# A kernel of attention, a gated FFN and a SoLU FFN: a new order of all its steps

## The chip, the cores and the metric

The kernel runs on one core of a Trainium2 chip. The metric is the device time of one execution in microseconds (us). Each measurement has several runs, and the median is taken.

## The reference

```python
scores = scale * np.matmul(rotate(q), rotate(k).transpose(0, 1, 3, 2))   # 2 batches, 8 heads, 576 tokens, 64 wide
attn = np.exp(scores - np.max(scores, axis=-1, keepdims=True))
attn = attn / (np.sum(attn, axis=-1, keepdims=True) + 1e-09)
x = np.matmul(attn, v)                            # -> 1152 tokens x 512
x = (x @ w_a) * (x @ w_b) @ w_out                 # 512 -> 1536 -> 512
h = x @ w_in                                      # 512 -> 1024
e = np.exp(h - np.max(h, axis=-1, keepdims=True))
solu = h * e / (np.sum(e, axis=-1, keepdims=True) + 1e-09)
ln = (solu - mu) / np.sqrt(var + 1e-06) * g_ln    # mean and variance over the 1024
out = ln @ w_out2                                 # 1024 -> 512
```

`rotate` is the rotary embedding by tables of cosines and sines. All data is float32.

## The kernel before, in words

**Precision.** Nearly every operand of a matrix product is kept as two parts, a high part (a rounded copy, made by ScalarE) and a low part (the rest, made by a subtraction on VectorE or GpSimd). A product takes three matmuls: high by high, high by low, low by high.

**Attention** works on eight units, each a pair of heads of one batch. A unit has nine tiles of 64 or 128 score rows, 72 tiles in all. Tile n passes through `qk.n` (scores, L444), `mx.n` (row maximum on VectorE, L453), `ex.n` (exponential on ScalarE, L461), `tp.n` (transposes, L474), `ph.n` and `pl.n` (high and low part, L488 and L492). Then come the products with V: `pv00_0.u` to `pv11_3.u` are, for four blocks of unit u, the first five matmuls, the last four (both L523), ScalarE's copy of one half of the result (L530) and VectorE's sum with the other half (L537). Beside this run the loads (`lk.u`, `lq.u`, `lv.u`, issued on SP's queue), the rotary steps (`rk`, `rq`) and the normalised rows of x (`xd`, L599 to L603).

**The gated FFN** computes part of its products by a Strassen-like scheme with seven products instead of eight, which needs sums of x: `s1`, `s3` and `sb` (L746, by way of L833 to L843) write the tiles `sums_f`. The columns of the first weight tiles are made plainly: `AB.f.t` (L715) fills a PSUM slot with both products, `ab.f.t` (L819) copies one to SBUF, `g.f.t` (L822) multiplies it by the other and so empties the slot. Weights come in by large loads (`ld`), are unpacked in integer steps (`p1` to `p4`, L173 to L181) and split (`hi`, `lo`, L192 and L195).

**The SoLU FFN** uses the same kind of scheme: `Q1` to `Q7` (L1130) are its products of six matmuls a piece, `q1` a copy of PSUM on ScalarE (L1137), `S..`, `Sh`, `Sl` the sums and their parts, `u` and `ul` those of the weights. Then `hx`, `he`, `hm`, `hs`, `hn` (L1158 to L1184) normalise a block of rows, `L` transposes it (L1192), `lh` and `ll` split it, and `O` (L1228) is the output product, whose weight's parts are made by `hj` (L792) and `lj` (L746).

**The order.** All of it is in one list of 1816 words, `SCHEDULE` (L35 to L141). A word is a step with its indices; a last `.1` puts the step on GpSimd where both engines can do it. The kernel walks through the list and calls the step of each word, and every engine's queue keeps the order in which the words issue to it:

```python
ctx.enter_context(tc.manual_schedule())                       # L205
...
def tt_(out_, a, b, op, eng=0):                               # L745
    (nc.vector, nc.gpsimd)[eng].tensor_tensor(out_, a, b, op=op)
...
def s1_a(k, eng=0):
    tt_(f_slot(0, k), _raw(x_part(k, 0)), _raw(x_part(2 + k, 0)), plus, eng)
def s3_a(k, eng=0):
    tt_(f_slot(2, k), _raw(x_part(k, 1)), _raw(x_part(k, 0)), sub, eng)
def s_b(j, k, eng=0):
    tt_(f_slot(j, k, 1), f_slot(j, k, 0), f_slot(j, k, 1), plus, eng)
...
for word in SCHEDULE.split():                                 # L1278
    name, *args = word.split(".")
    ...
    fn(*args)
```

So nothing but the list sets which instruction stands behind which on an engine; between engines, semaphores hold an instruction until its inputs are written and its buffer is free.

Of the kernel before, what the change touches and what calls it, by code (L numbers as in the profile page):

```python
# [20 lines left out]
B, H, S, D = 2, 8, 576, 64  # L21
# [14 lines left out]
wm1.0 rka0.0 ll.0 rka1.0 rka2.0 rkr0.0 rkr1.0 rkr2.0 rqx0.0 rqx1.0 rqx2.0 wm2.0 kha.0 kla.0 kA_0.0 rqa0.0 rqa1.0  # L36
kA_1.0 rqa2.0 qdx.0 qAx0.0 rkb0.0 qda.0 R_0.0 R_1.0 qA_0.0 qAh0.0 rkb1.0 rkb2.0 khb.0 rqb0.0 wm3.0 rqb1.0 qAh1.0
rqb2.0 cs.0 qAl0.0 qk.0 wm4.0 qAl1.0 qdb.0 R_2.0 mx.0 rq0.1 klb.0 lk.2 qk.1 mx.1 rq1.1 rq2.1.1 kB_0.0 rk0.1 ex.0
ex.1 qk.2 kB_1.0 mx.2 qB_0.0 qB_1.0 qd.1 qk.3 mx.3 rk1.1 tp.0 qB_2.0 tp.1 ex.2 ph.0 pl.0 ex.3 rk2.1.1 qk.4 mx.4
ph.1 t4A_0.0 rk0.2.1 lq.2 tp.2 t4A_1.0 t4A_2.0 kh.1 kl.1.1 lv.0 qA_0.1 ph.2 qA_1.1 qk.5 lv.1 pl.1 tp.3 ex.4 ph.3  # L40
mx.5 ex.5 vh.0 qk.6 pl.2 lk.3 vl.0.1 t4R_0.0 qA_2.1 rk1.2.1 t4R_1.0 rk2.2.1 kB_0.1 tp.4 mx.6 qk.7 pl.3 t4R_2.0
kB_1.1 tp.5 kA_0.1 mx.7 ph.4 pl.4 R_0.1 ex.6 qk.8 kA_1.1 mx.8 ph.5 pv00_0.0 pv00_1.0 tp.6 R_1.1 ex.7 R_2.1 ex.8
ph.6 qk.9 qk.10 lv.2 sa.0 pl.5 pv01_0.0 pv01_1.0 kh.2 rq0.2 mx.9 ex.9 qB_0.1 pv00_2.0 rq1.2.1 rq2.2.1 pv01_2.0
# [1277 lines left out]
```

## Time and profile before

| what | us |
|---|---|
| median of 3 runs | 482.96 |
| lowest and highest | 482.83, 483.72 |
| the profiled execution | 483.67 |
| its span | 481.9 |

The span runs from the first to the last instruction that the profile records; the execution's own time holds 1.77 us more. In the profile each instruction has a start and a duration. A time in square brackets behind a row is how long the engine stood idle before it, with the work whose end released it. PE is TensorE, DVE is VectorE, ACT is ScalarE, POOL is GpSimd, SP is the engine that issues most loads.

### The profile page before, as it was taken

The page shows a single profiled execution, that of the slowest core. Times are in us where ns is not written, and L with a number is a line of the kernel's source. Part 1 is how long each engine was busy: PE and PEld are TensorE (multiplying, and loading weights), DVE is VectorE, ACT ScalarE, POOL GpSimd, SP SyncE. Part 2 cuts the span into 40 slices and gives each one's busy share as a digit, 9 for nine tenths or more (in the row PEclk, how much of TensorE's full clock was granted, in tenths as well). Part 3 has the DMA queues.
Part 4 walks back from the last instruction along what each step waited for, and adds up shares of the span by engine and source line. Part 5 has one row for each costly group of instructions (what it writes and reads, how often), then busy time and mean ns, then how long its engine had stood idle before and what let it go on. Part 6 is the DMA issues. An engine that isn't in the chain of part 4 may idle for free.

```text
span 481.9 us, 8469 instructions
## 1 busy us (share of the span) xinstructions
PE 469.0 (97%) x3109; PEld 442.6 (92%) x3109; DVE 416.4 (86%) x634; ACT 344.6 (72%) x651; POOL 191.0 (40%) x157
## 2 busy tenths in 40 slices
PE   8899999999999989999999999999999999999997
PEld 7799999989989989999999999999999778888886
DVE  6999999999999699998998699787699999878671
ACT  4899999989898356787778887778886554434322
POOL 1799979789263200012152520222203586411100
PEclk9999999999999999999999999999999999999999
DMA  5532463241120415213235643454430220100002
GB/s 119 129 90 82 124 162 80 55 124 50 27 91 23 128 48 176 88 47 129 88 122 184 219 156 113 170 175 156 133 150 1 88 87 2 44 23 22 23 22 65
DMA packets 47351, 45.94 MB, mean 95 GB/s; under 512 B 24336, under 2 KB 41295, under 8 KB 46799
## 3 DMA queue, kind: packets, MB, share of 16 engines
q1 hardware_dynamic: 46366, 44.53, 30.2%
q10 hardware_dynamic: 944, 0.89, 0.6%
q8 instruction: 24, 0.39, 0.4%
q14 instruction: 17, 0.13, 0.1%
HBM read 39.01 MB, written 4.49 MB: 90 GB/s over the span
## 4 chain that ended last, share of the span: by engine, by line
PE 78%; DVE 10%; ACT 5%; POOL 3%; issue 2%; DMA 1%; SPq 0%; DVEq 0%; POOLq 0%; ACTq 0%
PE x L1012 16%; PE out L1228 10%; PE pb L942 9%; PE ab L715 6%; PE pc L942 6%; PE pa L942 5%; PE pv L523 5%; PE s L444 5%; PE h L1130 5%; PE t L474 3%; DVE nm L453 2%; DVE pT L492 2%; PE hc L1130 2%; PE lt L1192 2%; PE warm L639 1%
## 5 line engine op out<-in xcount | busy, mean ns | idle before, releaser
L1012 PE MATMUL x<-gs,wx 128*128 128x384 f32 x432 | 75.3, 334 | 0.0
L1012 PEld LDWEIGHTS x<-gs,wx 128*128 128x128 f32 x432 | 74.9, 188 | 0.3 <-issue 0.2
L444 PE MATMUL s<-kS,qS 128*128 128x288 f32 x320 | 58.7, 310 | 1.8 <-ACT e L461 1.5
L461 ACT ACTIVATE e<-s,nm 128x576 f32<-128x576 f32 x72 | 53.5, 744 | 5.0 <-DVE nm L453 4.5
L453 DVE TENSOR_REDUCE nm<-s 128x1 f32<-128x576 f32 x72 | 53.6, 751 | 0.7
L169 ACT ACTIVATE f<-f 128x1024 f32<-128x1024 f32 x48 | 50.9, 1061 | 1.0
L1228 PE MATMUL out<-wout,lnT 128*128 128x512 f32 (+1 forms) x240 | 50.9, 370 | 0.0
L444 PEld LDWEIGHTS s<-kS,qS 128*128 128x128 f32 x320 | 45.1, 189 | 4.3 <-ACT e L461 3.1
L492 DVE TENSOR_TENSOR pT<-t,pT 128x512 fp32r<-128x512 f32 x72 | 48.4, 683 | 0.7
L523 PE MATMUL pv<-pT,V 128*128 128x288 f32 x288 | 47.5, 303 | 1.2 <-DVE pT L492 0.6
L1228 PEld LDWEIGHTS out<-wout,lnT 128*128 128x128 f32 x240 | 41.6, 189 | 7.2
L488 ACT CAST pT<-t 128x512 fp32r<-128x512 f32 x72 | 41.5, 583 | 2.5 <-PE t L474 2.4
L474 PE MATMUL t<-ident,e 128*128 128x128 f32 x288 | 42.4, 274 | 0.7 <-DVE x L537 0.2
L523 PEld LDWEIGHTS pv<-pT,V 128*128 128x128 f32 x288 | 39.8, 188 | 2.3 <-issue 1.1
L715 PE MATMUL ab<-xT,wab 128*128 128x384 f32 x216 | 38.3, 335 | 1.6 <-DVE g L822 1.6
L715 PEld LDWEIGHTS ab<-xT,wab 128*128 128x128 f32 x216 | 37.3, 188 | 2.0 <-DVE g L822 1.9
L474 PEld LDWEIGHTS t<-ident,e 128*128 128x128 f32 x288 | 33.7, 141 | 2.8 <-DVE x L537 0.7
L179 DVE SCALAR_TENSOR_TENSOR f<-raw,f 128x1024 int32<-128x1024 int32 x26 | 35.0, 1347 | 0.4
L177 DVE SCALAR_TENSOR_TENSOR f<-raw,f 128x1024 int32<-128x1024 int32 x26 | 32.6, 1252 | 0.3
L942 PE MATMUL pb<-sums_x,wT 128*128 128x288 f32 x216 | 31.6, 295 | 0.0
L942 PE MATMUL pa<-xT,wB 128*128 128x288 f32 x216 | 31.6, 295 | 0.0
L942 PEld LDWEIGHTS pa<-xT,wB 128*128 128x128 f32 x216 | 29.7, 188 | 0.0
(212 smaller groups left out, 1021.3 us busy)
## 6 DMA issues: line engine op xcount, KB each, us to landing
raw<-in_moe_w_out_dram SPq DMA_DIRECT2D x10, 1024.0 KB, 4.9
raw<-in_moe_w_a_dram SPq DMA_DIRECT2D x12, 512.0 KB, 3.6
raw<-in_moe_w_b_dram SPq DMA_DIRECT2D x24, 256.0 KB, 4.2
raw<-in_moe_w_in_dram SPq DMA_DIRECT2D x4, 1024.0 KB, 5.6
kraw<-in_k_dram SPq DMA_DIRECT2D x16, 128.0 KB, 2.3
qd<-in_q_dram SPq DMA_DIRECT2D x16, 128.0 KB, 3.1
vraw<-in_v_dram SPq DMA_DIRECT2D x8, 256.0 KB, 3.0
wd<-f SPq DMA_DIRECT2D x4, 512.0 KB
```

The source lines that it names most:

```text
L169: act.activation(_raw(t), _raw(t), AF.Copy, scale=2.0 ** -SHIFT)
L444: nc.tensor.matmul(s[:, c, :KC], qS[u % 2][:, a, off:off + P], kS[u % 2][:, h, c * KC:(c + 1) * KC], start=(m == 0), stop=(m == last),)
L453: nc.vector.tensor_reduce(t, ps[n][:, :, :KC], axis=AX.XY, op=ALU.max, negate=True)
L461: nc.scalar.activation(t.rearrange("p (c n) -> p c n", c=2), ps.pop(n)[:, :, :KC], AF.Exp, bias=nm.pop(n), accum_out=sums[u][:, i:i + 1],)
L474: nc.tensor.transpose(t[:, j, :], e[n][:, j * P:(j + 1) * P], ident)
L488: nc.scalar.copy(hi, src)
L492: nc.vector.tensor_tensor(lo, src, _raw(hi), op=ALU.subtract)
L523: nc.tensor.matmul(o[:, :KC], w[:, h, 4 if m == 8 else m % 4].rearrange("p a d -> p (a d)"), t[:, m, c * KC:(c + 1) * KC], start=(m == 0), ...
L715: nc.tensor.matmul(pab[f, t][:, m, :CW], wf[:, a, (kk, 4 + (kk + 2) % 4)[m], :], xT[kk][:, xa, t * CW:(t + 1) * CW], start=(kk == a == xa ...
L942: nc.tensor.matmul(dst[:, c, :KC], w[:, a, k * P:(k + 1) * P], x(k, xa)[:, c * KC:(c + 1) * KC], start=(fresh and k == a == xa == 0), stop ...
L1012: nc.tensor.matmul(px[t, m][:, :CW], w[:, a], r[:, ga], start=(f == 0 and a == ga), stop=(f == NF - 1 and a == 1),)
L1228: nc.tensor.matmul(po[i, part][:, cols], lnT[i][:, la, kk, :], w[:, a, cols], start=(kk == la == a == 0), stop=(kk == NK2 - 1 and la == 1),)
```

## The change

The list `SCHEDULE` is replaced by another of 1816 words. It comes from a new search over the order of all steps on all engines, in which a longer time is laid out for each load in attention. Every step of the old list is in the new one. 49 words have another last index, so that their step moves between VectorE and GpSimd; the others only change places. Nothing else in the file differs.

```diff
 SCHEDULE = """
-wm1.0 rka0.0 ll.0 rka1.0 rka2.0 rkr0.0 rkr1.0 rkr2.0 rqx0.0 rqx1.0 rqx2.0 wm2.0 kha.0 kla.0 kA_0.0 rqa0.0 rqa1.0
+lv.0 wm1.0 rka0.0 cs.0 ll.0 wm2.0 rka1.0 rka2.0 rkr0.0 rkr1.0 rkr2.0 kha.0 rqx0.0 rqx1.0 rqx2.0 rqa0.0 kla.0
...
```

`lv.0`, the first load of V, moves from among the steps of tile 4 to the front of the list. The load of the first large weight, `ld.0`, moves from tile 29 to tile 11; those of k, q and v of the later units move by up to some ten tiles.

The end of attention on TensorE. `pv10` and `pv11` are two blocks of the last unit's product with V, `ab` the first product of the gated FFN. Before:

```order
L575 MATMUL rb_0_2559<-rr_2543,ident 64x128 x8
L575 MATMUL rb_1_2560<-rr_2543,ident 64x64 x2
L523 MATMUL pv_2571<-pT,V_2306 128x288 x9
L523 MATMUL pv_2583<-pT,V_2306 128x288 x9
L715 MATMUL ab_0_2511<-xT,wab_2250 128x384 x15
```

With the change:

```order
L575 MATMUL rb_0_2559<-rr_2541,ident 64x128 x8
L575 MATMUL rb_1_2560<-rr_2541,ident 64x64 x2
L523 MATMUL pv_2571<-pT,V_2248 128x288 x5
L523 MATMUL pv_2578<-pT,V_2248 128x288 x9
L523 MATMUL pv_2571<-pT,V_2248 128x288 x4
L715 MATMUL ab_0_2525<-xT,wab_2269 128x384 x15
```

The first block's last four matmuls now stand behind the whole second block.

The start of the gated FFN on GpSimd. `sums_f2` is written by `s3.1`, `sums_f0` by `s1`. Before:

```order
L345 CAST xT_71<-x0_6_2280 128x576
L593 TENSOR_TENSOR xT_71<-x0_6_2280,xT_71 128x576
L746 TENSOR_TENSOR sums_f2_2651<-xT_71 128x1152
L746 TENSOR_TENSOR xT_71<-sums_f0_2649,xT_71 128x576
L746 TENSOR_TENSOR wT5_3154<-tf5_3144,wT5_3154 128x1024
```

With the change:

```order
L345 CAST xT_71<-x0_6_2296 128x576
L593 TENSOR_TENSOR xT_71<-x0_6_2296,xT_71 128x576
L746 TENSOR_TENSOR sums_f2_2654<-xT_71 128x1152
L746 TENSOR_TENSOR sums_f0_2652<-xT_71 128x1152
L746 TENSOR_TENSOR tf4_3020<-f_2627,tf4_3020 128x256
```

`s1.1` has come from VectorE and stands right behind `s3.1`. On VectorE, in the same place, `sb.2.1` is the sum of `sums_f2` with itself, and the product `g0` behind it empties the first PSUM slot of `ab`. Before:

```order
L603 TENSOR_TENSOR xT_71<-x0_7_2522,xT_71 128x288
L746 TENSOR_TENSOR sums_f2_2651<-sums_f2_2651 128x576
L822 TENSOR_TENSOR g0_2646<-ab0_0_2511,a0_0_2667 128x384
L746 TENSOR_TENSOR sums_f2_2651<-xT_71 128x1152
L822 TENSOR_TENSOR g0_2646<-ab0_1_2669,a0_1_2723 128x384
```

With the change:

```order
L603 TENSOR_TENSOR xT_71<-x0_7_2511,xT_71 128x288
L746 TENSOR_TENSOR sums_f2_2654<-sums_f2_2654 128x576
L822 TENSOR_TENSOR g0_2649<-ab0_0_2525,a0_0_2672 128x384
L822 TENSOR_TENSOR g0_2649<-ab0_1_2678,a0_1_2703 128x384
L746 TENSOR_TENSOR sums_f0_2652<-sums_f0_2652 128x576
```

`s3.0`, which stood between the two products, comes later; `sb.2.1` and the first product keep their places.

The start of the SoLU FFN on TensorE. `h1` is the second block of rows, `h3` the third, `lt0` the transposes of the first normalised block, `out0` its output product. Before:

```order
L1130 MATMUL h1_4787<-hT00_4674,sx1_4753 128x512 x3
L1130 MATMUL h1_4787<-hT10_4746,sx1_4753 128x512 x3
L1192 MATMUL lt0_0_4868<-ident_65,et0_4808 128x128 x4
L1192 MATMUL lt0_1_4873<-ident_65,et0_4808 128x128 x4
L1130 MATMUL h1_4787<-wh2_4516,sx1_4753 128x512 x3
L1130 MATMUL h1_4787<-wh3_4706,sx1_4753 128x512 x3
L1130 MATMUL h3_4908<-wh0_4514,x2T_4411 128x512 x3
L1130 MATMUL h3_4908<-wh1_4709,x2T_4411 128x512 x3
L1228 MATMUL out0_0_4915<-wout0_4831,lnT0_4867 128x512 x6
```

With the change:

```order
L1130 MATMUL h1_4791<-hT00_4620,sx1_4758 128x512 x3
L1130 MATMUL h1_4791<-hT10_4749,sx1_4758 128x512 x3
L1130 MATMUL h3_4868<-wh0_4512,x2T_4410 128x512 x3
L1130 MATMUL h3_4868<-wh1_4653,x2T_4410 128x512 x3
L1192 MATMUL lt0_0_4880<-ident_65,et0_4806 128x128 x4
L1130 MATMUL h1_4791<-wh2_4515,sx1_4758 128x512 x3
L1130 MATMUL h1_4791<-wh3_4699,sx1_4758 128x512 x3
L1192 MATMUL lt0_1_4892<-ident_65,et0_4806 128x128 x4
```

Six matmuls of the third block (`h3`) have come ahead of the transposes, and six of the second stand between their two halves. On ScalarE the copy `q1.1` of the second block's PSUM result (L1137) goes ahead of the exponential of the first block (L1163), and on VectorE and GpSimd six of the sums of this stage change engine.

## Rows read from the trace of the kernel before

**Rows 1.** The page: busy time of each engine.
```profile
PE 469.0 (97%) x3109; PEld 442.6 (92%) x3109; DVE 416.4 (86%) x634; ACT 344.6 (72%) x651; POOL 191.0 (40%) x157
```

**Rows 2.** Busy time by stage: from:to, length, busy us (instructions), clock, DMA share, GB/s.
```profile
core 0: us, PE busy (x) PEld busy (x) DVE busy (x) ACT busy (x) POOL busy (x), PEclk, DMA share, GB/s
...
11.10:161.40 150.30, 145.72 (x1149) 137.60 (x1148) 145.89 (x245) 136.37 (x344) 108.58 (x85) 1.00 0.32 83
...
169.90:300.20 130.30, 130.10 (x925) 129.61 (x925) 118.37 (x147) 99.05 (x125) 25.16 (x15) 1.00 0.37 123
...
373.20:394.50 21.30, 20.52 (x95) 16.25 (x94) 20.19 (x32) 10.60 (x19) 14.65 (x13) 1.00 0.30 99
394.50:478.30 83.80, 83.78 (x425) 70.89 (x423) 60.95 (x110) 33.02 (x64) 22.58 (x28) 1.00 0.09 27
```

**Rows 3.** Timeline of the first 6 us: start, duration, engine, line, operation.
```profile
3.82 0.42 DVE L318 TENSOR_TENSOR t2k<-kraw,s_sb 128x256 f32<-128x256 f32 x1 [2.26 <-DMA s_sb<-in_rope_cs_dram]
...
4.30 0.39 SPq L631 DMA_DIRECT2D g_sb<-in_moe_g_ln_dram  x1
```

**Rows 4.** The page: loads of V, count, size, us from issue to landing.
```profile
vraw<-in_v_dram SPq DMA_DIRECT2D x8, 256.0 KB, 3.0
```

**Rows 5.** Timelines of VectorE and GpSimd at 98 us, and a like operation at 154.
```profile
97.97 1.84 DVE L173 TENSOR_SCALAR f<-f 128x1024 f32<-128x1024 f32 x1
...
97.84 1.43 POOL L325 TENSOR_TENSOR qd<-qd,t2q 128x576 f32<-128x576 f32 x1
...
153.77 0.68 DVE L173 TENSOR_SCALAR f<-f 128x1024 f32<-128x1024 f32 x1
```

**Rows 6.** Timeline of ScalarE at the end of attention.
```profile
161.58 0.39 ACT L530 COPY tmp7pv<-pv 64x288 f32<-64x288 f32 x1 [0.80 <-PE pv L523]
161.87 1.05 ACT L192 CAST wab<-f 128x1024 fp32r<-128x1024 f32 x1
```

**Rows 7.** Timelines of GpSimd, VectorE and TensorE at the start of the gated FFN.
```profile
165.90 2.66 POOL L746 TENSOR_TENSOR sums_f<-xT 128x1152 f32<-128x1152 f32 x1 [12.68 <-DVE xT L603]
...
168.60 0.76 DVE L746 TENSOR_TENSOR sums_f<-sums_f 128x576 f32<-128x576 f32 x1 [2.92 <-POOL sums_f L746]
...
169.88 2.35 PE L715 MATMUL ab<-xT,wab 128*128 128x384 f32 x12 [1.57 <-DVE g L822]
```

**Rows 8.** Timeline of GpSimd: three operations in a row at 141 us.
```profile
141.02 0.72 POOL L345 CAST V<-vraw 128x640 fp32r<-128x640 f32 x1
141.82 1.56 POOL L363 TENSOR_TENSOR V<-vraw,V 128x640 fp32r<-128x640 f32 x1
143.34 1.43 POOL L593 TENSOR_TENSOR xT<-x,xT 128x576 fp32r<-128x576 f32 x1
```

**Rows 9.** Timelines at 389 us, and all VectorE instructions of line 1184.
```profile
389.10 1.35 DVE L1184 TENSOR_SCALAR et<-et,mv,rs 128x1024 f32<-128x1024 f32 x1 [0.21 <-POOL rs L1179]
...
389.16 0.74 POOL L746 TENSOR_TENSOR sx<-sf,sx 128x256 fp32r<-128x256 f32 x1
...
L1184 DVE TENSOR_SCALAR et<-et,mv,rs x9: 805/812/1351, 389.1 to 467.0; 128x1024 f32<-128x1024 f32 x9
```

**Rows 10.** Timeline of TensorE from 382 us: groups of matmuls (x is their number).
```profile
382.23 1.52 PE L1130 MATMUL hc<-hT,sx 128*128 128x512 f32 x6
383.90 1.98 PE L1130 MATMUL h<-hT,sx 128*128 128x512 f32 x6 [0.16 <-ACT h L1137]
385.72 1.53 PE L1130 MATMUL hc<-hT,x2T 128*128 128x512 f32 x6
387.09 1.52 PE L1130 MATMUL h<-wh,x2T 128*128 128x512 f32 x6
388.45 1.52 PE L1130 MATMUL h<-hT,sx 128*128 128x512 f32 x6
390.51 1.12 PE L1192 MATMUL lt<-ident,et 128*128 128x128 f32 x8 [0.54 <-DVE et L1184]
...
394.49 1.75 PE L1228 MATMUL out<-wout,lnT 128*128 128x512 f32 x7
```

**Rows 11.** Timeline of GpSimd: the low parts of the last output weight.
```profile
389.86 5.18 POOL L746 TENSOR_TENSOR wout<-wout 128x1024 fp32r<-128x1024 f32 x2
```

More of the change, by code (lines that the diff above doesn't have):

```diff
@@ new lines @@
+mx.18 pl.15 ex.18 vh.2 lv.3 tp.16 vl.2.1 qd.3 rk1.4.1 rk2.4.1 rs_0.1 lq.4 pv00_3.1 pv01_3.1 rs_1.1 tp.17 qk.20
+rs_2.1 rq0.4.1 kA_0.3 mx.19 qB_2.2 ph.16 pl.16 t4B_0.1 ex.19 qk.21 mx.20 ph.17 pl.17 tp.18 kA_1.3 t4B_1.1
+rq1.4.1 qA_0.3 t4B_2.1 pv10_0.1 ex.20 pv10_1.1 qk.22 tp.19 ph.18 mx.21 qA_1.3 pl.18 ex.21 lv.4 qA_2.3 mx.22
+qk.23 pv10_2.1 ph.19 ex.22 tp.20 pv10_3.1 ph.20 pv11_0.1 mx.23 ex.23 pl.19 pv11_1.1 vh.3 tp.21 t4R_0.2 pl.20
+pv11_2.1 t4R_1.2 pv11_3.1 t4R_2.2 qk.24 mx.24 kB_0.3 t4A_0.2 lk.5 xa.1.1 tp.22 ph.21 pl.21 qk.25 tp.23 kB_1.3
@@ new lines @@
+qk.33 qA_2.4 ph.28 kh.5 pl.28 pv11_0.2 tp.30 mx.33 ph.29 pl.29 ex.32 pv11_1.2 vh.4 pv10_2.2 ph.30 qk.34 pv10_3.2
+t4R_0.3 kB_0.4 pv11_2.2 pv11_3.2 ex.33 t4R_1.3 t4A_0.3 kB_1.4 qk.35 mx.34 t4A_1.3 tp.31 pl.30 tp.32 ex.34 ph.31
+t4A_2.3 ph.32 xa.2.1 xb.2 R_0.4 t4R_2.3 R_1.4 pl.31 pv00_0.3 rq2.5.1 qd.5 p0.0 lk.6 pv00_1.3 pv00_2.3 mx.35
+ex.35 qk.36 tp.33 ph.33 R_2.4 sa.3 pv01_0.3 pl.32 pv01_1.3 qB_0.4 pv01_2.3 lq.6 mx.36 ex.36 xc.2.1 pv00_3.3
+qB_1.4 qk.37 pl.33 tp.34 ph.34 rs_0.3 rs_1.3 kl.5.1 pv01_3.3 tp.35 qk.38 rs_2.3 mx.37 ex.37 qB_2.4 kA_0.5
@@ new lines @@
+mx.58 pl.54 qA_1.7 tp.55 tp.56 qA_2.7 pv11_0.5 ex.57 ex.58 qk.59 ph.55 p3.0 pv10_2.5 pl.55 ph.56 pv11_1.5
+pv11_2.5 mx.59 ex.59 pl.56 qk.60 mx.60 pv10_3.5 tp.57 ph.57 xb.4 t4R_0.6 t4R_1.6 ex.60 qk.61 pv11_3.5 mx.61
+kB_0.7 kB_1.7 qk.62 pl.57 mx.62 t4A_0.6 tp.58 xa.5.1 t4R_2.6 t4A_1.6 t4A_2.6 ph.58 pl.58 tp.59 ph.59 R_0.7 ex.61
+pv00_0.6 tp.60 R_1.7 pv00_1.6 qk.63 p4.0 vh.7 R_2.7 pl.59 ex.62 qk.64 ld.1 pv01_0.6 sa.6 hi.0 pv01_1.6 ph.60
+mx.63 ex.63 mx.64 xc.4.1 rs_0.6 pv00_2.6 qB_0.7 pv01_2.6 qB_1.7 pl.60 pv00_3.6 pv01_3.6 qB_2.7 ex.64 qk.65 mx.65
@@ new lines @@
+pl.69 A0.0.0 pl.70 A0.0.1 rs_1.7 xb.6 pv01_2.7 A0.0.2 rs_2.7 xc.6.1 tp.71 t4B_0.7 ph.71 t4B_1.7 pv01_3.7 p2.1
+pl.71 rb.7 pv10_0.7 t4B_2.7 pv11_0.7 pv11_1.7 pv10_1.7 pv10_2.7 A0.0.3 pv11_2.7 p3.1 p4.1 ld.3 hi.1 pv11_3.7
+pv10_3.7 xd0.7 xd1.7 to_ffn ld.2 s3.1.1 A0.1.0 A0.1.1 A0.1.2 A0.1.3 ab.0.0 sb.2.1 sh.2.1 s1.1.1 g.0.0 AB.0.1
+ab.0.1 g.0.1 AB.0.2 sb.0.1 lo.1 sh.0.1 s1.0 AB.1.0 pa.2 ab.0.2 sb.0.0 s2a.1 g.0.2 s3.0 pb.2 pc.2 pa.3 p2.2
+ab.1.0 s2b.1 sh.1.1 p3.2 g.1.0 p4.2 ld.4 sb.2.0 pb.3 pc.3 p2.3 hi.2 lo.2 AB.1.1 sh.0.0 ab.1.1 AB.1.2 ab.1.2
@@ new lines @@
+o4.7 g0.7 t4.9.1 sc.10.0 P7.8 sc.10.1 so.10 P6.8 pa.11 th.9 pb.11 pc.11 o7.8 o6.8 o2.8 tl.9.1 P4.8 pa.12 p2.11
+pb.12 p3.11 p4.11 g1.7 pc.12 P5.8 P1.9 o5.8 P3.8 o1.9 P2.9 bh.10 o2.9 t1.10.1 o4.8 P7.9 p2.12 p3.12 p4.12 P6.9
+t2.10 sc.12.1 sc.12.0 o7.9 g1.8 t4.10.1 ld.13 th.10 g0.8 P4.9 o6.9 P5.9 bl.10.1 o4.9 o5.9 pa.13 pb.13 ld.14
+pc.13 P1.10 g0.9 o1.10 p2.13 p3.13 so.12 pa.14 p4.13 pb.14 ld.15 tl.10.1 t1.11 t2.11 P7.10 o7.10 P3.9 pc.14
+p2.14 bh.11 t4.11 P6.10 o6.10 P4.10 p3.14 p4.14 P5.10 th.11 bl.11 hi.14 P2.10 o2.10 tl.11 pa.15 pb.15 o4.10
@@ new lines @@
+p4.19 ld.21 gl.0.7 X.0.6 X.1.3 gh.1.4 lo.18 hi.19 pa.20 gl.1.4 gh.0.8 pb.20 X.0.7 X.1.4 gh.1.5 gl.0.8.1 lo.19
+pc.20 gh.0.9 gl.1.5 p2.20 p3.20 p4.20 X.1.5 ld.22 pa.21 pb.21 pc.21 gl.0.9 p2.21 X.0.8 gh.1.6 gh.0.10 X.0.9
+gl.0.10 gl.1.6 X.1.6 X.0.10 p3.21 sc.20.0 sc.20.1 so.20 p4.21 ld.23 gh.1.7 gh.0.11 gl.0.11.1 sc.21.1 X.0.11
+sc.21.0 so.21 gh.1.8 xh.0.0 pa.22 gl.1.8 pb.22 pc.22 gh.1.9 gl.1.7.1 X.1.7 xl.0.0 X.1.8 p2.22 gl.1.9 p3.22 X.1.9
+xh.0.3 xl.0.3 xh.0.1 xh.0.2 xl.0.2 gh.1.10 gl.1.10.1 pa.23 gh.1.11 p4.22 pb.23 ld.24 gh.2.0 xl.0.1 pc.23
@@ new lines @@
+uh.1.0 xh.2.2 ri.12 lo.24 ri.20 S1b.1 Sh.1.1 u2.1 ul.1.0 xl.1.2 Sh.1.3 Sl.1.3.1 S2a.1 S3a.3 S2b.1 Sh.1.2 u4.1
+uh.1.1 H.0.1 H.0.2 H.0.3 Q1.1 Sl.1.2.1 q1.1 S1a.3.1 xl.2.2 S1b.3.1 hx.0 he.0 S4a.1.1 Q7.1 q7.1 ul.1.1 S3b.3.1
+Q6.1 hj.20 Sl.1.1.1 Q4.1 q6.1 ri.10 Q2.1 Q5.1 S4b.1.1 Sh.1.4 xh.2.3 hj.10 hm.0 hs.0 lj.10.1 hj.12 xl.2.1 Q1.3
+Sl.1.4 q1.3 hn.0 xl.2.0 L.0.0 q5.1 Q3.1 L.0.1 q4.1 lh.0.0 lj.12.1 Sh.3.3 xl.2.3 ll.0.0 hx.1 he.1 hx.2 hm.1
+O.0.0.0 he.2 Sl.3.3.1 Q7.3 Q1.5 hm.2 S2a.3.1 S2b.3.1 Sh.3.1 Sh.3.2 Sl.3.2.1 Q6.3 q7.3 lh.0.1 Q4.3 lj.20.1 hs.1
@@ L142 @@
+O.8.0.1 st.7.0 O.8.1.1 st.8.1 O.8.0.2 O.8.1.2 st.8.2
 """
```

174 lines of the change are left out of this document (69 added, 105 removed).

## The prediction

> **What bounds the kernel now.** I read the page's busy times first, then a table of busy time by stage, then the timelines at the seams between stages. The page says that TensorE is busy for 97% of the span, VectorE for 86%, ScalarE for 72% and GpSimd for 40% [rows 1]. That is an average over stages that differ. The table by stage tells them apart [rows 2]. In attention (11.1 to 161.4 us) VectorE is the fullest engine: 145.89 of 150.30 us, with TensorE at 145.72 right beside it. From 169.9 us on, in the gated FFN, TensorE is busy for 130.10 of 130.30 us, so no order of the steps can win there. At the seam into the SoLU FFN (373.2 to 394.5 us) it works 20.52 of 21.30 us, with VectorE at 20.19, and the seam before the gated FFN comes below. The granted clock is 1.00 in all of these rows, the upper level of 2.4 GHz. So the time can change in three places: in attention through VectorE, and at the two seams through whatever TensorE waits for.
>
> The profiled execution took 483.67 us, 0.71 us above the median of the runs, 482.96 us; its span is 481.9 us, and 1.77 us lie around it. The sum below is made against 483.67 and ends with these 0.71 taken off. A measurement of this kernel can tell about 0.2% from no change, 0.97 us.
>
> **Start and attention.** The change puts the first V load (one transfer of 256 KB and two small ones) at the head of SP's queue and moves later loads by whole tiles. SP's queue has a hole there: its next issue starts only at 4.30 us, when VectorE has cleared the tile for it, while VectorE's first operation waits until 3.82 us for the sine table, which ScalarE's queue issued at the very start [rows 3]. The V load needs 3.0 us from issue to landing [rows 4], so issued in the hole it lands behind that table. I take 0. The ends are 0 and, if V's packets pushed back what VectorE works on next, a part of those 3.0 us; an estimate of that part is 1.0 us, a third, since V's 256 KB are then in flight beside the small loads and not ahead of all of them. The other loads of attention are issued earlier or later by tiles of about 2 us (150.30 us for 72 tiles [rows 2]), and in the table VectorE never has room for a wait of that size, so I take 0 for them too.
>
> In attention VectorE does the same work before and after, except that two rotary steps of equal length change places with GpSimd. Its 4.41 us without work [rows 2] are the most that a better order could find, and one operation there is held up: an operation of 0.68 us took 1.84 us [rows 5], because GpSimd had begun an operation on SBUF tiles 0.13 us earlier, at 97.84 us, and held it until 99.27 us. VectorE's operation ended at 99.81 us, 0.54 us after GpSimd's. So the two exclude each other while both read SBUF, and the blocked one ends its own length less 0.14 us behind the other. The new order moves such meetings about and I cannot place each: I take 0, with ends of -2.5 us (this 1.16 us won back and a third of the idle time) and +2.5 us (two more such meetings).
>
> **The end of attention.** The last PV product used to be two blocks of nine matmuls. Now the first is cut: five, then the other block's nine, then the remaining four. So both of ScalarE's copies come behind the last matmul instead of one. The second copy follows the first by 0.29 us in the chain (161.58 to 161.87 us is the step from such a copy to the next operation on ScalarE [rows 6]). I take +0.29 us; the ends are 0 and 0.39 us, the copy's length.
>
> **The seam into the gated FFN** is where I expect most. GpSimd's sum s3.1 runs from 165.90 us for 2.66 us to 168.56; VectorE's sum sb.2.1 needs it, starts at 168.60 and ends at 169.36; VectorE's product g0.0 is queued behind it, and TensorE stands for 1.57 us until that has emptied a PSUM slot [rows 7]. The change puts GpSimd's next sum, s1.1, of the same shape and so 2.66 us, right behind s3.1; before, it was VectorE's, later. It needs nothing that s3.1 makes. Of three GpSimd operations in a row, the second reads what the first wrote and starts 0.08 us after its end; the third doesn't and starts 0.04 us before the recorded end of the second [rows 8]. So s1.1 starts at about 168.52 us and VectorE's sb.2.1, released at 168.60, meets it on SBUF tiles and is held until 171.18 us. It then ends at 171.18 + 0.76 - 0.14 = 171.80 us instead of 169.36: **+2.44 us** for g0.0 and for TensorE behind it. The ends are 0 (sb.2.1 goes first) and 2.66 us (the whole operation). Nothing takes these 2.44 us back: TensorE has no idle time in the next stage in which to catch up [rows 2].
>
> How near a thing this is shows in another place: VectorE's normalisation at 389.10 us had begun 0.06 us before GpSimd's operation at 389.16 us, and yet took 1.35 us where 0.81 is the median, ending 0.55 us behind GpSimd's end [rows 9]. So GpSimd wins even when it starts some 0.06 us later. The Trainium skill's SBUF — State Buffer, section "SBUF: two separate sides", says that of a VectorE operation with two SBUF inputs and a GpSimd operation the one that starts first keeps the shared ports for the whole instruction. The row at 389.10 us goes against its order by those 0.06 us, and the measurement decides. Did s1.1 start 0.08 us after the end of s3.1 rather than before it, that rule would let sb.2.1 go first and the seam would cost nothing, while by the row GpSimd would still hold it.
>
> **The gated FFN.** Of the 49 steps that change between VectorE and GpSimd 23 lie in this stage. TensorE covers them as long as each is ready before its products; it was idle for 0.20 us in 130.30 [rows 2]. I take 0; the ends are -0.2 and +1.0 us (one meeting such as the one at 97.97 us falling on a weight that is due).
>
> **The seam into the SoLU FFN.** Six matmuls follow each other by 1.36 us when nothing is late (387.09 to 388.45 us [rows 10]). The step from 382.23 to 383.90 us is 0.31 longer, that from 383.90 to 385.72 0.46, that from 388.45 to 390.51 0.70: together 1.47 us. The first two come with a PSUM copy on ScalarE that stands behind the exponential, the third is TensorE waiting for the normalised tile. The change puts that copy first, and puts six matmuls of another product, which need no such tile, ahead of the transposes: that covers the waits. What is late next is the last weight: its two low parts keep GpSimd until 389.86 + 5.18 = 395.04 us [rows 11]. The second half of the first output product reads them; before, it began six matmuls after 394.49, at 395.85 us, and now, with its first half one block earlier, it can begin no sooner than the weight is there. So of the 1.47 us only 395.85 - 395.04 = 0.8 is kept: **-0.8 us**. The ends are -1.47 us (GpSimd, with fewer sums ahead, has the weight done sooner) and +1.0 us, since four sums of about 0.7 us go to VectorE there, which has only 1.1 us to spare in that stage [rows 2].
>
> **The tail.** From 394.5 us on TensorE is busy for 83.78 of 83.80 us and VectorE for 60.95 [rows 2], so the sums that change engine there are covered: 0.
>
> **The sum.** 0 + 0.29 + 2.44 + 0 - 0.8 = +1.93 us on 483.67 gives 485.60 us, and less 0.71 us **484.9 us**.
>
> **The rivals.** *VectorE goes first at the seam into the gated FFN.* The place is sb.2.1 against s1.1; the point that decides is which of them has the tiles when s3.1 ends. For it: the two are released within about 0.1 us of each other. Against it: the pair at 97.84 us and that at 389.16 us, both GpSimd's. Then the seam costs nothing, s1.1 is needed only later, and the sum is 0.29 - 0.8 = -0.51: 483.16, less 0.71, 482.4 us, not slower than before.
>
> *The new order gains in attention too.* VectorE isn't blocked at the seam, wins 1.5 us in attention (the 1.16 us of the blocked operation and 0.3 us of idle time) and the whole 1.47 us at the SoLU seam: 0.29 - 1.5 - 1.47 = -2.68, which gives 480.3 us. For it: attention is the longest stage in which TensorE has idle time, and a longer time for loads could only show there. Against it: VectorE's work is unchanged and its idle time is 3% of the stage.
>
> *The meetings of VectorE and GpSimd multiply.* To the forecast comes a wait of 2.4 us in attention, two meetings of about 1.2 us each: 487.3 us. For it: VectorE has no slack there, so each counts in full, and GpSimd is busy for 108.58 of 150.30 us. Against it: in those 150 us of the old order I found one.
>
> *The longer time for loads does nothing* holds in all four cases: none gives the moved loads a price, because the trace of before shows no wait on VectorE in attention that they could take away.
>
> **Chances and range.** The forecast 0.40, VectorE first 0.25, gain in attention as well 0.20, more meetings 0.15. The forecast's own range is 484.2 to 486.7 us by its ends at the SoLU seam. Faster than 482.0 us are the third case and a third of the second (0.28); within 0.2% are the rest of the second and a little of the first (0.19); slower than 483.9 us is what is left (0.53). The range of 8 in 10 reaches from 480.6 us, which leaves out over half of the third case, to 487.6 us, which leaves out under half of the fourth: some 0.18 outside.
>
> **What would show it.** Right: VectorE's sum of 128x576 behind s3.1 takes over 3 us in the new profile, with a GpSimd sum of 2.66 us beside it, and TensorE's wait there is about 4 us instead of 1.57; the copies after the last PV product lie within 0.4 us of each other; TensorE's groups that are now spread from 382 to 390 us keep the 1.36 us pace, and a wait for the weight appears in the first output product. Wrong: the sum takes its 0.76 us; VectorE's stage from 11.1 us on is shorter or longer by over 1 us; or the stage after 169.9 us shows TensorE waiting.

## The result, and the profile after

The changed kernel takes 487.88 us (median of 6 runs, 486.32 to 488.52) beside 483.25 us for the kernel before: a ratio of 1.0088, 95% interval 1.0071 to 1.0105. It is slower, as forecast, but by 4.3 us (by the ratio) where I had forecast 1.9. Its profiled execution took 487.91 us, with a span of 486.0 us and a mean granted clock of 0.991; the kernel before had 1.000. Of the changed kernel's six executions four have a mean clock of 0.991 or 0.992 and take 487.85 to 488.52 us, two have 0.996 and take 486.32 and 486.70 us.

The page of the kernel after: the busy times, and TensorE's group of the first products of the gated FFN (busy, mean ns of one, idle before and its releaser). The last row is the same group on the page of the kernel before.

```profile
PE 471.6 (97%) x3109; PEld 445.9 (92%) x3109; DVE 412.1 (85%) x631; ACT 345.7 (71%) x651; POOL 194.7 (40%) x160
...
L715 PE MATMUL ab<-xT,wab 128*128 128x384 f32 x216 | 40.6, 349 | 4.2 <-DVE g L822 4.2
...
L715 PE MATMUL ab<-xT,wab 128*128 128x384 f32 x216 | 38.3, 335 | 1.6 <-DVE g L822 1.6
```

The busy times hardly differ from those before [rows 1]. What differs is one wait, of 4.2 us instead of 1.6, and that the same 216 matmuls keep TensorE busy for 2.3 us longer. The stages of the kernel after follow (the third number from the end of a row is the clock). Up to 172.10 us they are cut at the events of before [rows 2]; the last three rows are cut only near them, since the orders differ there, and don't hold the same matmuls:

```profile
11.10:161.00 149.90, 146.19 (x1151) 138.17 (x1149) 145.57 (x246) 135.90 (x343) 108.49 (x85) 1.00 0.32 83
161.00:169.00 8.00, 6.90 (x40) 6.58 (x39) 3.22 (x9) 3.00 (x6) 3.23 (x2) 1.00 0.68 218
169.00:172.10 3.10, 0.00 (x0) 0.00 (x0) 3.07 (x2) 0.46 (x1) 1.99 (x1) 0.72 0.33 114
172.10:177.10 5.00, 4.98 (x16) 4.98 (x17) 4.33 (x6) 2.36 (x4) 0.00 (x0) 0.50 0.00 0
177.10:302.90 125.80, 124.66 (x889) 124.19 (x889) 107.67 (x137) 95.66 (x121) 23.24 (x15) 1.00 0.36 123
302.90:376.50 73.60, 73.60 (x431) 73.39 (x430) 60.69 (x77) 57.62 (x80) 15.89 (x11) 1.00 0.38 135
376.50:398.60 22.10, 22.10 (x109) 19.05 (x108) 20.36 (x34) 13.16 (x23) 13.05 (x12) 1.00 0.28 96
```

Three things stand in this table. From 169.00 to 172.10 us TensorE does nothing, and the granted clock falls while it waits. From 172.10 to 177.10 us it is 0.50, the lower level of 1.2 GHz: TensorE is busy nearly all the time with 16 matmuls. And the seam into the SoLU FFN, where TensorE had stood for 0.78 us and run in gaps, is now dense.

The seam into the gated FFN, in the timelines of TensorE, VectorE and GpSimd of the kernel after:

```profile
160.95 6.95 PE L715 MATMUL ab<-xT,wab 128*128 128x384 f32 x39
172.12 16.10 PE L715 MATMUL ab<-xT,wab 128*128 128x384 f32 x78 [4.23 <-DVE g L822]
...
165.08 0.46 DVE L603 TENSOR_TENSOR xT<-x,xT 128x288 fp32r<-128x288 f32 x1 [0.50 <-ACT xT L602]
168.46 3.15 DVE L746 TENSOR_TENSOR sums_f<-sums_f 128x576 f32<-128x576 f32 x1 [2.92 <-POOL sums_f L746]
171.53 0.54 DVE L822 TENSOR_TENSOR g<-ab,a 128x384 f32<-128x384 f32 x1
...
165.77 5.22 POOL L746 TENSOR_TENSOR sums_f<-xT 128x1152 f32<-128x1152 f32 x2 [13.90 <-DVE xT L603]
```

These answer to [rows 7]. GpSimd's two sums run on without a gap until 170.99 us. VectorE's sum sb.2.1, released at 168.46, is recorded at 3.15 us instead of 0.76 and ends at 171.61 us, 0.62 us behind GpSimd; the product behind it releases TensorE at 172.12 us, 2.24 us later than before, and TensorE has waited 4.23 us instead of 1.57.

### The profile page after: what moved, and what is told of

Read it like the earlier page. It is cut to its first block, busy times and chain, and to the rows that moved or that the text cites. A ratio compares the mean times of both kernels' runs of the same rounds, so it can differ in the third digit from the quotient of the medians.

```text
span 486.0 us, 8473 instructions
## 1 busy us (share of the span) xinstructions
PE 471.6 (97%) x3109; PEld 445.9 (92%) x3109; DVE 412.1 (85%) x631; ACT 345.7 (71%) x651; POOL 194.7 (40%) x160
## 4 chain that ended last, share of the span: by engine, by line
PE 75%; DVE 10%; ACT 7%; DMA 3%; POOL 2%; issue 2%; SPq 0%; POOLq 0%; ACTq 0%; DVEq 0%
PE x L1012 15%; PE out L1228 10%; PE pb L942 9%; PE ab L715 7%; PE h L1130 6%; PE pa L942 6%; PE pc L942 5%; PE pv L523 4%; PE s L444 3%; DVE nm L453 3%; ACT e L461 3%; PE t L474 2%; PE hc L1130 2%; DVE pT L492 2%; PE lt L1192 2%
## 5 line engine op out<-in xcount | busy, mean ns | idle before, releaser
L715 PE MATMUL ab<-xT,wab 128*128 128x384 f32 x216 | 40.6, 349 | 4.2 <-DVE g L822 4.2
L715 PEld LDWEIGHTS ab<-xT,wab 128*128 128x128 f32 x216 | 39.6, 198 | 4.6 <-DVE g L822 4.5
L523 PEld LDWEIGHTS pv<-pT,V 128*128 128x128 f32 x288 | 39.9, 188 | 1.4 <-issue 0.6
L177 DVE SCALAR_TENSOR_TENSOR f<-raw,f 128x1024 int32<-128x1024 int32 x26 | 32.6, 1252 | 0.4
L179 DVE SCALAR_TENSOR_TENSOR f<-raw,f 128x1024 int32<-128x1024 int32 x26 | 31.8, 1222 | 0.6
```

Of the source, the lines that this page charges most:

```text
L523: nc.tensor.matmul(o[:, :KC], w[:, h, 4 if m == 8 else m % 4].rearrange("p a d -> p (a d)"), t[:, m, c * KC:(c + 1) * KC], start=(m == 0), ...
L715: nc.tensor.matmul(pab[f, t][:, m, :CW], wf[:, a, (kk, 4 + (kk + 2) % 4)[m], :], xT[kk][:, xa, t * CW:(t + 1) * CW], start=(kk == a == xa ...
```

## The experiments

All experiments but two change only the list of words; a2 and c3 also add transposes on TensorE whose result nothing reads. Where an experiment's fence shows line numbers that are 5 lower than before, its list took five lines fewer. Ratios are to the kernel before, run beside each.

| run | median, us | ratio | 95% interval |
|---|---|---|---|
| a1_sum_on_vector | 484.03 | 1.0013 | 0.9999 to 1.0027 |
| a2_keep_busy | 486.10 | 1.0044 | 1.0028 to 1.0060 |
| a3_sum_behind_product | 482.43 | 0.9972 | 0.9960 to 0.9984 |
| b1_sum_on_gpsimd | 488.29 | 1.0090 | 1.0073 to 1.0106 |
| b2_new_attention | 485.30 | 1.0033 | 1.0021 to 1.0046 |
| b3_new_solu | 481.70 | 0.9959 | 0.9946 to 0.9971 |
| b4_loads | 486.18 | 1.0049 | 1.0031 to 1.0067 |
| b5_loads | 483.62 | 1.0001 | 0.9989 to 1.0013 |
| b6_sum_behind_product | 482.17 | 0.9968 | 0.9956 to 0.9980 |
| c1_att_and_solu | 483.08 | 0.9990 | 0.9975 to 1.0004 |
| c2_sum_behind_product | 481.06 | 0.9943 | 0.9932 to 0.9955 |
| c3_keep_busy | 482.05 | 0.9965 | 0.9952 to 0.9978 |

The theory after the result: GpSimd's s1.1 holds VectorE's sb.2.1, the product behind it releases TensorE late, and behind its long wait TensorE is granted the lower clock. The first rival: the clock falls for another reason than the wait. The second: the loss needs more of the new order than this one sum.

### One sum, put in and taken out

b1_sum_on_gpsimd, in the old order:

```diff
-to_ffn s3.1.1 A0.1.0 ... lo.1 AB.1.0 s1.1 sh.2.1
+to_ffn s3.1.1 s1.1.1 A0.1.0 ... lo.1 AB.1.0 sh.2.1
```

> The kernel before with s1.1 alone put on GpSimd right behind s3.1. Theory: this one word makes the loss: sb.2.1 takes 3.1 us, TensorE waits about 4 us and is slowed behind it, 2.4 + 2.4 us more than before, about 488 us. Rival (the meeting needs the rest of the new order): the time of before, 483.3 us, or less by up to 1.35 us of VectorE's work.

Measured: 488.29 us, 1.0090, the whole loss of the changed kernel and a little more. Timelines of its TensorE, VectorE and GpSimd, and its group of the first products:

```profile
172.60 7.56 PE L710 MATMUL ab<-xT,wab 128*128 128x384 f32 x33 [3.96 <-DVE g L817]
...
165.55 0.46 DVE L598 TENSOR_TENSOR xT<-x,xT 128x288 fp32r<-128x288 f32 x1 [0.50 <-ACT xT L597]
168.93 3.15 DVE L741 TENSOR_TENSOR sums_f<-sums_f 128x576 f32<-128x576 f32 x1 [2.93 <-POOL sums_f L741]
...
166.24 5.23 POOL L741 TENSOR_TENSOR sums_f<-xT 128x1152 f32<-128x1152 f32 x2 [12.69 <-DVE xT L598]
...
L710 PE MATMUL ab<-xT,wab 128*128 128x384 f32 x216 | 39.9, 344 | 4.0 <-DVE g L817 4.0
```

From the last VectorE operation on x to TensorE's going on it is 172.60 - 165.55 = 7.05 us here, 172.12 - 165.08 = 7.04 us in the changed kernel, and 169.88 - 165.22 = 4.66 us before. One word costs 2.39 us of waiting. The products behind the wait account for 1.6 us more (39.9 us instead of 38.3) in this execution, whose mean clock is 0.996; four of the six have 0.993. So the rest of the 0.90% (4.4 us), some 2.0 us, fits the clock, though by subtraction only. The second rival falls.

a1_sum_on_vector, in the new order:

```diff
-sb.2.1 sh.2.1 s1.1.1 g.0.0 AB.0.1 ab.0.1 g.0.1 AB.0.2 sb.0.1 lo.1 sh.0.1
+sb.2.1 sh.2.1 g.0.0 AB.0.1 ab.0.1 g.0.1 AB.0.2 lo.1 s1.1 sb.0.1 sh.0.1
```

> The changed kernel with one sum, s1.1, put back on VectorE, behind the product that empties the PSUM slot and behind the weight's low part. Theory (GpSimd's s1.1 holds VectorE's sb.2.1, TensorE waits 4.23 us instead of 1.57 and is granted the lower clock level behind that wait): sb.2.1 takes its 0.76 us again, the wait goes back to about 1.5 us, the clock stays at 1.00, and the time falls by 2.4 us of waiting and 2.4 us of slow matmuls, to about 483 us. Rival (the clock falls for another reason, such as the end of attention): only the 2.4 us of waiting go, about 485.5 us.

Measured: 484.03 us. In the profiled execution sb.2.1 takes 0.76 us again and TensorE's wait is 1.84 us, not 1.57: the new attention leaves TensorE with its last matmul sooner, but not the sum that it then waits for. Of twelve executions six show a clock of 0.995 or 0.996 and take 484.97 us at the median; the other six, at 0.999 or 1.000, take 483.2. So by the ratios 0.75% or 3.6 us are won back, and what is left of the loss lies in the six executions with the lower clock.

### The clock by itself

a2_keep_busy adds work to the changed kernel between AB.0.1 and AB.0.2:

```diff
+    def busy():
+        t = pools["a"].tile([P, 2, 512], F32, tag="a", name="busy")
+        for i in range(36):
+            nc.tensor.transpose(t[:, 0, (i % 4) * P:(i % 4 + 1) * P], ident, ident)
```

> The changed kernel with 36 transposes of the identity, whose result nothing reads, put into TensorE's queue where it waits for the slot (36 x 0.109 = 3.9 us at the upper level). Theory (the clock falls because TensorE stands idle for 4.2 us): sb.2.1 still takes 3.15 us, TensorE goes on with the products at the same 172.1 us, but at the upper level, so 2.4 us are won: about 485.5 us. Rival (the clock falls anyway, or only useful work counts): 487.9 us or more.

Measured: 486.10 us; by the ratios 0.44% less than the changed kernel, 2.1 us. Timelines of TensorE and VectorE, busy times with the clock, and the group of the first products:

```profile
169.10 4.09 PE L1276 MATMUL busy<-ident 128*128 128x128 f32 x36
173.52 6.70 PE L710 MATMUL ab<-xT,wab 128*128 128x384 f32 x37 [0.32 <-DVE g L817]
...
169.83 3.17 DVE L741 TENSOR_TENSOR sums_f<-sums_f 128x576 f32<-128x576 f32 x1 [2.92 <-POOL sums_f L741]
...
167.90:172.10 4.20, 4.20 (x36) 4.16 (x35) 2.27 (x1) 0.00 (x0) 4.20 (x2) 1.00 0.75 250
173.50:178.50 5.00, 4.98 (x28) 4.98 (x29) 4.34 (x6) 2.74 (x6) 0.00 (x0) 1.00 0.00 0
...
L710 PE MATMUL ab<-xT,wab 128*128 128x384 f32 x216 | 38.3, 336 | 0.3 <-DVE g L817 0.3
```

VectorE is held just as long, and TensorE goes on with its products no sooner: 173.52 us is 7.07 us behind the last VectorE operation on x, at 166.45. But the clock stays at 1.00, in all six executions, and the first five microseconds of the products hold 28 matmuls instead of 16. The group takes 38.3 us again, 2.3 less than in the changed kernel. The clock falls because TensorE stands, and it costs 2.1 us by the medians, 2.3 in the profiled executions. The first rival falls. The Trainium skill's TensorE: Matmul & The Clock Gate, section "HAM oscillation — how this bites in real kernels", describes this: a wait of TensorE for its data lets the gate fall to half rate, and the matmuls behind the wait run slowly. The trace agrees, with 0.50 from 172.10 to 177.10 us behind the wait of 4.23 us.

c1_att_and_solu takes the new list up to `to_ffn`, the old one up to the product `X.2.4`, and the new one from there; six words that lie on different sides of these seams in the two lists go with the new one.

> The new order in attention and, from the last products of the gated FFN on, in the SoLU FFN; the old order in the gated FFN between them. Theory (the new order is worth 1.7 us at the seam into the SoLU FFN and 0.1 us at the end of attention, and all of its loss lies in the gated FFN): about 481.5 us, faster than before. Rival (the gain at the SoLU seam depends on sums done earlier in the gated FFN): 483 us.

Measured: 483.08 us, no different from before. Five of twelve executions have a clock of 0.998 or more and take 481.85 us at the median, near the 481.5 expected; seven, at 0.995 or 0.996, take 483.87. The profiled one is of the first kind. To see whether the wait makes the difference, c3_keep_busy puts 14 of those transposes into the wait of c1:

> The mixed order with 14 transposes of the identity, whose result nothing reads, in TensorE's wait of 1.9 us. Theory (half of the executions of the mixed order lose 2 us to the lower clock level behind that wait of 1.9 us): every execution shows a clock of 0.998 or more, and the median falls to about 482.0 us. Rival (the lower clock comes from another place): times spread as before, median 483.1 us.

Measured: 482.05 us, all five executions at 1.000 and within 1.45 us of each other, where c1's spread over 2.92. That is what the theory says; but c3 ran on another chip than c1, and c1 wasn't run there. b2_new_attention is c1 without the new SoLU order:

> The new order in attention alone, the old one behind it. Theory (the new attention hands over 0.14 us sooner, yet lengthens TensorE's wait from 1.57 to 1.87 us and so brings the lower clock into half of the executions): no faster than before, 483.5 to 484.7 us. Rival (attention gains by itself): 482.5 us or less.

Measured: 485.30 us, slower than expected, with all seven executions at 0.996. Busy times of its profiled execution around the wait, and its group of the first products:

```profile
167.10:169.10 2.00, 0.22 (x2) 0.00 (x0) 1.22 (x3) 0.49 (x1) 0.75 (x1) 1.00 1.07 372
169.10:173.10 4.00, 3.94 (x14) 3.94 (x15) 4.00 (x5) 0.00 (x0) 0.00 (x0) 0.57 0.08 26
...
L715 PE MATMUL ab<-xT,wab 128*128 128x384 f32 x216 | 39.8, 345 | 1.8 <-DVE g L822 1.8
```

Here the lower clock came behind a wait of 1.84 us, and the products behind it took 1.5 us longer (39.8 instead of 38.3). The new attention, taken alone, loses 0.33%, 1.6 us: the wait is only some 0.3 us longer, the rest goes with the clock. The length of the wait doesn't decide by itself: in c1's profiled execution it was 1.87 us, and the clock stayed at 1.00. Why c1, with nearly the same list up to the end of the gated FFN, has the lower clock in seven executions of twelve and b2 in seven of seven, these runs don't settle; the two also ran on different chips.

### The wait by itself

If VectorE's product is only late because it stands behind a sum that waits for GpSimd, the place of that sum is the thing to change. c2_sum_behind_product does so in c1, and puts s3.0 behind it:

```diff
-ab.0.0 AB.0.1 sb.2.1 g.0.0 AB.0.2 ab.0.1 s3.0 g.0.1 ab.0.2
+ab.0.0 AB.0.1 g.0.0 AB.0.2 ab.0.1 g.0.1 sb.2.1 s3.0 ab.0.2
```

> The mixed order (new attention, old gated FFN, new SoLU FFN) with VectorE's sum sb.2.1 put behind the two products that empty the PSUM slots, and s3.0 behind it. Theory: TensorE's wait there has one cause, that VectorE's product is queued behind a sum that waits for GpSimd; with the product ahead the whole wait of 1.9 us goes and the clock has no reason to fall: 483.1 less 1.9, and less about 1.2 for executions of the mixed order with a lower granted clock, about 480.0 us. Rival (the low part of the next weight, now later on VectorE, stops TensorE in its place): 482 to 483 us.

Measured: 481.06 us, 0.9943, the fastest of all and faster than both kernels. TensorE's timeline:

```profile
161.31 19.46 PE L715 MATMUL ab<-xT,wab 128*128 128x384 f32 x111
181.18 11.04 PE L715 MATMUL ab<-xT,wab 128*128 128x384 f32 x62 [0.41 <-DVE g L822]
```

111 matmuls follow each other where the wait was. 1.0 us of the forecast is missing; 0.4 us of it is the wait that is left at 181 us, where VectorE's next product stands behind an unpacking step.

b6_sum_behind_product makes the same move, of sb.2.1 and s3.0, in the old order, where it is the only change:

> The kernel before with sb.2.1 put behind the two products that empty the PSUM slots, nothing else. Theory: its wait of 1.57 us goes and 0.6 us come back at 181 us, where VectorE's next product is late: 1.0 us faster, about 482.6 us. Rival (no gain without the new attention): 483.6 us.

Measured: 482.17 us, 0.9968. The place of two words wins 1.5 us (the list moves s3.0 behind the second product too, which the expectation leaves out). a3_sum_behind_product leaves s1.1 on GpSimd in the changed kernel and moves only sb.2.1, with the step sh.2.1 that rounds its result:

```diff
-ab.0.0 sb.2.1 sh.2.1 s1.1.1 g.0.0 AB.0.1 ab.0.1 g.0.1 AB.0.2
+ab.0.0 s1.1.1 g.0.0 AB.0.1 ab.0.1 g.0.1 sb.2.1 sh.2.1 AB.0.2
```

> The changed kernel, s1.1 still on GpSimd, with sb.2.1 put behind the two products. Theory: sb.2.1 is still held for 2.4 us, but the products ahead of it aren't, so the wait of 4.23 us goes, the clock stays at 1.00, and what is left is a wait of about 1.7 us for the next weight's low part, which stands behind the held sum: 487.9 - 4.2 - 2.4 + 1.7 = 483.0 us. Rival (the products, which read PSUM and SBUF, are held by GpSimd too): 487 us or more.

Measured: 482.43 us. Its VectorE and TensorE:

```profile
168.50 0.56 DVE L822 TENSOR_TENSOR g<-ab,a 128x384 f32<-128x384 f32 x1 [1.67 <-ACT a L819]
168.97 3.43 DVE L746 TENSOR_TENSOR sums_f<-sums_f 128x576 f32<-128x576 f32 x2
172.32 1.21 DVE L195 TENSOR_TENSOR wab<-f,wab 128x1024 fp32r<-128x1024 f32 x1
...
173.59 6.69 PE L715 MATMUL ab<-xT,wab 128*128 128x384 f32 x37 [1.14 <-DVE wab L195]
```

The product, which reads PSUM and SBUF, takes its 0.56 us at 168.50 us while GpSimd is at work; only the sums behind it are held. What is left is 1.14 us for the next weight's low part, as expected in kind. By the ratios this move wins 1.16%, 5.6 us, more than the whole loss: the loss came from what stood behind the held sum.

### The seam into the SoLU FFN, and the loads

b3_new_solu has the new order from `X.2.4` on only, with five of the words named above.

> The kernel before with the new order in the SoLU FFN alone. Theory (the stalls of 1.7 us between 380 and 392 us are filled, and the output product's weight isn't late): 1.7 us faster, about 482.0 us. Rival (my forecast, that the weight's low parts keep half of it): 0.8 us faster, about 482.8 us.

Measured: 481.70 us, 0.9959, 2.0 us faster. The gain there is whole.

b4_loads moves the loads in the old order to the tiles of the new one:

> The kernel before with the loads of attention and the first weight load moved to the tiles at which the changed kernel issues them, at most to two tiles ahead of their first use; all else in the old order. Theory (VectorE doesn't wait for loads, so their place is worth nothing): 483.3 us, within 0.5. Rival (earlier loads lift a wait or push back others): a difference of 1 us or more either way.

Measured: 486.18 us, a miss. TensorE and SP's queue in its profiled execution:

```profile
37.47 0.63 PE L377 MATMUL qtqA<-ident,qd 128*128 128x128 f32 x4 [2.83 <-DMA qd<-qd]
...
30.08 1.25 SPq L287 DMA_DIRECT2D qd<-in_q_dram  x2
31.37 1.27 SPq L292 DMA_DIRECT2D qd<-in_q_dram  x2
32.73 0.66 SPq L332 DMA_DIRECT2D qd<-qd  x1
```

My edit had put one load of q ahead of the copy that makes the second half of another unit's q tile. Its four issues take SP's queue from 30.08 to 32.64 us, and TensorE waits 2.83 us for the copy behind them. b5_loads moves eleven loads, none past such a copy, V and the first 1 MB of weights among them:

> The kernel before with eleven loads moved as in the changed kernel (all of V, the first large weight, two of q, one of k), those whose new place isn't behind their first use in the old order; no load passes a copy that feeds TensorE. Theory (the 3 us that the other arrangement of loads lost come from one q load put ahead of the copy of q, not from the loads of V or the weight): 483.5 us, within 0.5. Rival (1 MB of weights in attention pushes the small loads back): 485 us or more.

Measured: 483.62 us, 1.0001. The places of these eleven loads are worth nothing by themselves, either way. b5 leaves other loads of b4 in their old places as well, so that the q load made b4's loss rests on the wait of 2.83 us in its trace.

## Why the prediction was right, and by how much not

**What bounds the kernel** held in part. The time changed at the two seams, but also in the gated FFN between them, where I had said that no order can win: it can lose there, by 2.3 us at the lower clock and 1.1 us in two waits. Attention has no clear part: TensorE's first product of the gated FFN that is in one piece starts at 160.95 us instead of 161.38, but the last VectorE operation on x starts between 164.51 and 166.45 us in the profiled executions with the new attention, so single executions don't tell. What the new attention did to the time, by b2, is the longer wait behind it and the clock.

**Start, 0 us.** The V load did go into the hole at 2.35 us. VectorE's first operation began at 3.75 us instead of 3.82, but two later ones waited for the small loads on ScalarE's queue:

```profile
2.35 0.62 SPq L297 DMA_DIRECT2D vraw<-in_v_dram  x1
...
5.59 0.23 DVE L318 TENSOR_TENSOR t2k<-kraw,s_sb 128x64 f32<-128x64 f32 x1 [0.49 <-DMA kraw<-in_k_dram]
...
7.62 0.43 DVE L318 TENSOR_TENSOR t2q<-qd,s_sb 128x256 f32<-128x256 f32 x1 [0.52 <-DMA qd<-in_q_dram]
```

The first of these waits, of 0.21 to 0.50 us, is in all ten profiled executions that issue the V load first and in none of the four others. That is up to half of my upper end of 1.0 us on VectorE at that place, and b5, which has it at 0.45 us, shows that it doesn't reach the time.

**The end of attention, +0.29 us**, was right. In the kernel after both copies run in one row from 161.15 us for 0.69 us and VectorE's sum starts at 161.87:

```profile
161.15 0.69 ACT L530 COPY tmp7pv<-pv 64x288 f32<-64x288 f32 x2 [3.59 <-PE pv L523]
...
161.87 0.83 DVE L537 TENSOR_TENSOR x<-pv,tmp7pv 64x288 f32<-64x288 f32 x2 [0.83 <-ACT tmp7pv L530]
```

From the copy's start to the sum it is 0.72 us; before, with the last copy at 161.58 us [rows 6] and the sum at 162.00, it was 0.42. TensorE doesn't wait for these copies, but the sum that it waits for later comes behind them: this is the wait of 1.84 us instead of 1.57 in b2.

**The seam into the gated FFN, +2.44 us**, was right in its mechanism and size: 2.39 us by b1. What failed is that the sum ends there: I took a wait of TensorE at its length, put nothing for what it does to the clock, and gave no reason. That the granted clock was 1.00 in all the rows of before, beside a wait of 1.57 us, spoke for nothing longer than that. The missing term is +2.1 us, by a2.

**The gated FFN, 0 us with an upper end of +1.0,** came out at about +1.1 us by two new waits of TensorE, neither of them a meeting of VectorE and GpSimd:

```profile
266.36 1.86 PE L942 MATMUL pc<-xT,wT 128*128 128x288 f32 x12 [0.40 <-ACT p L955]
...
292.86 1.33 PE L942 MATMUL pa<-xT,wB 128*128 128x288 f32 x8 [0.74 <-ACT c L963]
```

ScalarE copies a product out of PSUM, and the next product into that bank now comes up before the copy is done. I had looked at the inputs of the products only, not at when their banks come free. Both waits are in the four profiled executions with the new order there (the changed kernel, a1, a2, a3) and in none with the old one. With them one of my own signs of being wrong came true, that the stage behind the seam shows TensorE waiting.

**The seam into the SoLU FFN, -0.8 us,** was too small: TensorE and GpSimd of the kernel after, beside [rows 10, 11], and in the last row GpSimd's step `rs` before:

```profile
386.51 1.52 PE L1130 MATMUL h<-wh,x2T 128*128 128x512 f32 x6
387.87 1.52 PE L1130 MATMUL hc<-hT,sx 128*128 128x512 f32 x6
...
394.67 1.52 PE L1130 MATMUL h<-wh,x2T 128*128 128x512 f32 x6
396.03 0.60 PE L1192 MATMUL lt<-ident,et 128*128 128x128 f32 x4
...
398.21 3.02 PE L1228 MATMUL out<-wout,lnT 128*128 128x512 f32 x12
...
393.29 0.55 POOL L1179 TENSOR_TENSOR rs<-mv,mhalf 128x1 f32<-128x1 f32 x1 [1.03 <-DVE mv L1177]
394.10 5.25 POOL L746 TENSOR_TENSOR wout<-wout 128x1024 fp32r<-128x1024 f32 x2 [0.26 <-ACT wout L792]
...
388.51 0.55 POOL L1179 TENSOR_TENSOR rs<-mv,mhalf 128x1 f32<-128x1 f32 x1 [1.42 <-DVE mv L1177]
```

From 387.87 us to the output product it is 10.34 us; before, 382.23 to 394.49 us, 12.26. The gain is 1.92 us, more than the 1.47 us I had as the far end, since the transposes, split by six matmuls, cost TensorE less as well. My reason for halving it failed: the weight's low parts are done at 399.35 us, and the second half of the output product, six matmuls after 398.21, starts at about 399.6. GpSimd began on the weight 6.23 us after 387.87 us, where before it was 7.63 us after 382.23. Fewer sums on GpSimd explain only a part of this: in both orders it stood idle before its small step `rs` until VectorE's normalisation had got so far (1.42 us before, 1.03 after), and that point came 0.86 us sooner; the other 0.54 us lie between `rs` and the weight, where a sum of 0.74 us is gone.

**The sum.** The forecast's +0.29, +2.44, 0 and -0.8 make +1.93 us. Measured terms: +0.29, +2.39, +2.1 (the clock), +1.1 and -1.9 make +4.0 us, and the ratio says 4.3. The two profiled executions, whose spans differ by 4.1 us, agree: TensorE came to the seam 0.43 us sooner, waited 2.66 us longer, and lost 2.3 us at the lower clock and 1.1 us in the two waits, and the SoLU seam gave back 1.92 us, together +3.7 of these 4.1 us. Two of my errors, the bank waits and the SoLU seam, came near to cancelling, which was luck; the clock is what is left. The range ended at 487.6 us: the ratio puts the kernel inside, at 1.0088 x 482.96 = 487.2 us, and the median of its own measurement, 487.88 us, just outside. That end of the range stood for more meetings in attention, not for the clock.

**The rivals.** VectorE's sb.2.1 did not go first in any of the three kernels that queue it there with s1.1 directly behind s3.1 on GpSimd (the changed kernel, a2, b1). The gain in attention did not come. My reading of the pair at 389 us [rows 9], that GpSimd wins even from behind, rests on one pair of recorded starts 0.06 us apart, of an operation on one tile and two columns (`et`, `mv`, `rs`) where sb.2.1 adds two tiles, and was not put to the test: s1.1 began before the sum was released, so rule and row gave the same.

## What to carry to other kernels

A wait of TensorE has two prices: its length, and the slower matmuls that follow when the clock falls during it or just behind it; here 2.4 us more of waiting brought 2.1 us at the lower clock on top. On an engine that works in order, put the operation that frees another engine's buffer ahead of one that waits for a third engine: moving two words that way won 1.5 us in the kernel before. And before giving GpSimd a long operation on SBUF, ask which VectorE operation will be released while it runs, and what stands behind that.

## What the runs showed of the hardware that was not expected

In kernels whose profiled execution shows a wait of 1.84 or 1.87 us on TensorE, the lower clock came in every execution of one (b2, seven of seven) and in about half of two others (a1, six of twelve; c1, seven of twelve); before, with 1.57 us, the mean clock stayed at 0.998 or more in the executions beside them. 36 transposes whose result nothing reads keep the clock up as useful matmuls do, and so won 2.1 us here in a wait that they don't shorten. And where a load of 256 KB goes out on SP's queue at about the same time as loads of 16 KB on ScalarE's queue, VectorE waits 0.21 to 0.50 us for one of these in all ten profiled executions; without it, in none of four.
